# An attention and Fourier kernel: score banks taken strictly by turns, the maxima's transpose one piece later, the first pairs' row loads spread

## The chip, the core and the metric

The kernel runs on one core of a Trainium2 chip. The metric is the device time of one execution in microseconds (us). A core has five engines that run side by side, each with its own queue in order: PE (TensorE: matrix multiplies; PEld is its weight load), DVE (VectorE), ACT (ScalarE), POOL (GpSimd) and SP (SyncE, which here issues every DMA). PE writes to PSUM, which has eight banks; DVE and ACT read the results from there. A bank can be filled again only when the last reader of its earlier content is done.

## The reference

Two independent layers are computed and laid side by side in the output. Layer A is attention over 2048 positions, 32 heads of 18 channels, in 4 segments of 512, each with a softmax of its own, a linear memory carried from segment to segment, a gate per head, and an output projection. Layer B is the real part of a two-dimensional Fourier transform, written as matrix products.

```python
for s in range(N):                                   # N = 4 segments
    qs, ks, vs = q[:, :, s], k[:, :, s], v[:, :, s]
    logits = jnp.einsum("bhqd,bhkd->bhqk", qs, ks) * scale + mask
    p = _softmax(logits, axis=-1)
    a_dot = jnp.einsum("bhqk,bhkd->bhqd", p, vs)
    pq = phi(qs)
    num = jnp.einsum("bhld,bhde->bhle", pq, M)
    den = jnp.einsum("bhld,bhd->bhl", pq, z)[..., None] + 1e-6
    outs.append(g * (num / den) + (1.0 - g) * a_dot)
    pk = phi(ks)
    M = M + jnp.einsum("bhld,bhle->bhde", pk, vs)
    z = z + jnp.einsum("bhld->bhd", pk)
...
a = jnp.einsum("bsd,ed->bse", x, dft_hid_re)
b = jnp.einsum("bsd,ed->bse", x, dft_hid_im)
y = jnp.einsum("ts,bse->bte", dft_seq_re, a) - jnp.einsum("ts,bse->bte", dft_seq_im, b)
```

`mask` holds -1e9 wherever the key comes after the query, so a block of 128 rows needs only the columns up to its own.

## The kernel before

Float32 operands are split in a high and a low part, and each product is made of three. The program has three stretches. First the projections of layer A for the four segments (up to about 228 us): q, k and v go through DRAM (`qd`, `kd`, `vd`). Then, up to about 960 us, the attention of 128 heads-by-segment is woven into the matrix products of layer B. Last comes the rest of layer B and the output projection.

The weave is written out by hand. `dense()` is a generator that emits layer B a few matmuls at a time: `hidden` (L531) and `sequence` (L550), whose operands come as chunks: `c_load` (L372) issues the DMA into `craw`, `c_cut` (L380) splits it on ACT (L387, `chi`) and POOL (L392, `clo`), two chunks before `chunk` (L526) hands it to PE. `attention()` (L806) is a generator of pieces: for each step p it yields eight times, and after each piece `tick()` runs what `later(n, ...)` has put down for that tick, then as much of `dense()` is emitted as the weights in `SLOTS` (L804) ask for. So each engine's order is fixed, and all its waits are met in that order.

A pair is two heads, 2p and 2p+1; four heads (two pairs) are a group G, whose stacked rows lie in `qs_bufs[G % 4]` and `ks_bufs[G % 4]`. `stack_load(G, a, b, each)` (L419) loads rows a to b-1 of twelve, `each` of them per tick, each 72 KB. The even head of a pair first has its row minima taken (`s_fill`, three parts: PE writes scores, L665, DVE reduces them, L671), and later its transposed scores filled and turned to exponentials (`t_fill`, three parts: PE L739 to L746, ACT L749 and L750). For that the minima must become rows: `maxima(G)` (POOL, L712) cuts them in three bf16 parts, `maxima_transpose(G)` (L720) turns them on PE (tile `trm`, L722), ACT copies them out (tile `mt`, L724), and two DMAs (`qs<-mt`) write them as three more rows of the stack, in the tick after. The odd head (`f_fill`, L680) has its scores filled the plain way, exponentials by ACT (`f_exp`, L694) and the transpose by DMA (`f_turn`, L710).

One step p emits, piece by piece (the lag in pairs in brackets):

| piece | what it emits |
|---|---|
| 0 | low part of the even head's exponentials (4), `f_exp` part 2 (3), `s_fill` part 0, `f_split_hi` on ACT (3) |
| 1 | `t_fill` parts 0 and 1 (3), low split on POOL |
| 2 | for even p `maxima_transpose(p/2 - 1)`; then `s_fill` part 1, low split on DVE |
| 3 | `pv` of the even head (4), `s_fill` part 2, the mask on POOL (3) |
| 4 | `f_fill` part 1 (2), `t_fill` part 2 (3), for odd p `maxima` |
| 5 | `f_turn` (3), `stack_load` for a group to come, `f_fill` part 0 (2), `t_hi` on ACT |
| 6 | `pv` of the odd head (4), `f_fill` part 2 (2), `f_exp` part 1 (2) |
| 7 | `f_exp` part 0 (2), the output of pair p-4 |

PSUM in this stretch (pool `ps2`, L484): tag `s` has two banks (the three `s_fill` parts and `f_fill` parts 1 and 2), tag `t` has two (`t_fill`, `f_fill` part 0, `trm`), `d` three for layer B, `pv` one. With `bufs=2` under one tag the pool decides which of the two banks a fill takes. In the built program 29 of the 320 fills with tag `s` take the bank that the fill right before them had; they are all `s_fill` part 1 behind `s_fill` part 0. Among the fills with tag `t` none does.

## Time and profile before

| what | value |
|---|---|
| time of three runs | 1048.86, 1049.44, 1051.51 us (median 1049.44) |
| the profiled execution's own time | 1052.35 us |
| its span, first to last instruction | 1050.6 us |
| PE busy | 1015.7 us (97%), 9464 matmuls |
| DVE, ACT, POOL busy | 723.0, 712.7, 623.1 us |
| mean granted PE clock | 0.990 |
| DMA | 194.26 MB, 185 GB/s on average; all issued by SP |

The span is some 1.75 us shorter than the time of the same execution; the rest lies before the first and behind the last instruction. Busy times of different engines overlap. What ends up in the time is what PE, the fullest engine, does not get done: its own work, the times it stands and waits, and the stretches in which the clock granted to it is lower.

### The profile page before, as it was taken

The numbers are of one execution on the slowest core, as the hardware profiler recorded it, in microseconds if no ns is written. First come the engines' busy times: TensorE is split into PE (matmuls) and PEld (weight loads), VectorE is DVE, ScalarE is ACT, GpSimd is POOL, SyncE is SP. The second block draws the span as 40 slices with busy tenths as digits, with TensorE's granted clock in tenths as the row PEclk, the third lists the DMA queues.
The fourth block names the chain that finished last, engine by engine and source line by source line (L and its number), as shares of the span: only waits on it lengthen the run. The fifth ranks groups of instructions, "written<-read, shape, count | busy, mean of one in ns | idle before, by whom it ended". The sixth has DMA issues, their size and how long they took to land.

```text
span 1050.6 us, 25818 instructions
## 1 busy us (share of the span) xinstructions
PE 1015.7 (97%) x9464; PEld 949.4 (90%) x9464; DVE 723.0 (69%) x1903; ACT 712.7 (68%) x1654; POOL 623.1 (59%) x668
## 2 busy tenths in 40 slices
PE   9999999998999999999999999999899999999998
PEld 7989999898998999999898899999899989889998
DVE  6546556564777777878777767778677778887343
ACT  7656575653876878777787777777577766776233
POOL 3567575864765666766666766666566656766000
PEclk9999999999999999999999999999899999999999
DMA  7526164367667898999999988799999999978574
GB/s 253 177 75 208 64 206 142 118 240 173 144 159 182 181 207 202 207 196 220 206 187 209 204 174 162 155 204 199 202 209 212 216 216 212 237 148 197 142 211 140
DMA packets 287263, 194.26 MB, mean 185 GB/s; under 512 B 210208, under 2 KB 242336, under 8 KB 287136
## 3 DMA queue, kind: packets, MB, share of 16 engines
q1 hardware_dynamic: 287136, 192.61, 77.8%
q8 instruction: 74, 1.21, 0.5%
q14 instruction: 53, 0.43, 0.1%
HBM read 106.64 MB, written 43.78 MB: 143 GB/s over the span
## 4 chain that ended last, share of the span: by engine, by line
PE 73%; ACT 9%; DMA 7%; DVE 4%; POOL 3%; SPq 3%; issue 2%; POOLq 0%; ACTq 0%; DVEq 0%
PE d L494 26%; PE qk L77 6%; PE d L77 6%; PE s L665 5%; PE qk L229 5%; PE v L77 4%; DMA craw<-cT 4%; PE pv L781 3%; ACT pf L694 2%; PE d L540 2%; PE d L541 2%; PE d L542 2%; ACT hl L701 2%; PE pv L782 2%; PE m L313 2%
## 5 line engine op out<-in xcount | busy, mean ns | idle before, releaser
L671 DVE CUSTOM_DVE_ANT_0 s<-s,causal 128x128 f32<-128x128 f32 (+3 forms) x512 | 251.5, 499 | 124.1 <-PE s L665 113.0
L392 POOL TENSOR_TENSOR clo<-craw,chi 128x512 fp32r<-128x512 f32 x158 | 214.6, 1358 | 121.6 <-ACT chi L387 89.0
L494 PE MATMUL d<-wide,chi 128*128 128x288 f32 x1408 | 270.2, 309 | 0.0
L494 PEld LDWEIGHTS d<-wide,chi 128*128 128x128 f32 x1408 | 215.9, 192 | 1.3 <-issue 0.2
L494 PE MATMUL d<-wide,clo 128*128 128x288 f32 x704 | 180.8, 324 | 0.0
L705 POOL TENSOR_TENSOR hl<-pf,hl 128x768 f16<-128x768 f32 x64 | 113.2, 1768 | 79.7 <-ACT hl L701 62.5
L665 PE MATMUL s<-ks,qs 108*128 108x128 bf16 (+3 forms) x512 | 135.4, 306 | 5.9 <-DVE negm L671 4.9
L694 ACT ACTIVATE pf<-s,nb 128x128 f32<-128x128 f32 (+3 forms) x256 | 128.1, 526 | 6.2
L749 ACT ACTIVATE phi<-t 128x384 f16<-128x384 f32 x128 | 62.2, 486 | 103.2 <-PE t L746 103.2
L387 ACT ACTIVATE chi<-craw 128x512 fp32r<-128x512 f32 x160 | 100.6, 629 | 43.0 <-DMA craw<-cT 24.5
L494 PE MATMUL d<-ab,chi 128*128 128x288 f32 x640 | 126.1, 306 | 0.0
L494 PEld LDWEIGHTS d<-wide,clo 128*128 128x128 f32 x704 | 121.2, 193 | 2.7 <-issue 1.8
L764 DVE TENSOR_TENSOR plo<-pf,phi 128x384 f16<-128x384 f32 (+1 forms) x128 | 112.3, 877 | 0.0
L750 ACT ACTIVATE pf<-t 128x384 f32<-128x384 f32 (+1 forms) x192 | 100.2, 522 | 3.0 <-PE t L739 2.9
L494 PEld LDWEIGHTS d<-ab,chi 128*128 128x128 f32 x640 | 98.6, 189 | 0.8 <-issue 0.3
L701 ACT ACTIVATE hl<-pf 128x768 f16<-128x768 f32 (+1 forms) x128 | 87.4, 729 | 2.0
L540 PE MATMUL d<-wide,chi 128*128 128x288 f32 x256 | 85.2, 333 | 2.7 <-DVE wide L55 2.7
L494 PE MATMUL d<-ab,clo 128*128 128x288 f32 x320 | 84.9, 314 | 0.0
L665 PEld LDWEIGHTS <-qs 108*128 108x128 bf16 x512 | 41.4, 98 | 41.6 <-issue 25.3
L764 POOL TENSOR_TENSOR plo<-pf,phi 128x384 f16<-128x384 f32 x64 | 60.1, 940 | 31.6 <-ACT pf L750 31.1
L541 PE MATMUL d<-wide,chi 128*128 128x288 f32 x256 | 76.2, 298 | 0.0
L542 PE MATMUL d<-wide,clo 128*128 128x288 f32 x256 | 76.1, 297 | 0.0
(196 smaller groups left out, 2546.8 us busy)
## 6 DMA issues: line engine op xcount, KB each, us to landing
craw<-cT SPq DMA_DIRECT2D x128, 256.0 KB
ks<-kd SPq DMA_DIRECT2D x192, 72.0 KB
qs<-qd SPq DMA_DIRECT2D x192, 72.0 KB
craw<-xtT SPq DMA_DIRECT2D x32, 320.0 KB
out<-y SPq DMA_DIRECT2D x31, 288.0 KB
vd<-vs SPq DMA_DIRECT2D x16, 440.0 KB
vst<-vd SPq DMA_DIRECT2D x32, 220.0 KB
qd<-p SPq DMA_DIRECT2D x16, 384.0 KB
```

The lines of the kernel that those rows point to most:

```text
L77: pe.matmul(o, a, b, start=n == 0, stop=n == len(terms) - 1)
L387: act.activation(hi, raw[:, :4], AF.Copy)
L392: engine.tensor_tensor(lo, raw[:, :4], hi.bitcast(F32), OP.subtract)
L494: pe.matmul(o[h], a, b[:, h * 288:h * 288 + 288], start=start, stop=stop)
L540: pe.matmul(o, xh[:, k], wl[k][:, cs], start=k == 0, stop=False)
L665: pe.matmul(o[:, c:c + w], q[:, i * P:w], k[:, :w], start=True, stop=True)
L671: dve.tensor_tensor_reduce(o[:, c:c + w], o[:, c:c + w], CAUSAL[0][:, L - w:], scale=scale, scalar=-LOWEST, op0=OP.add, op1=OP.min, accum_ ...
L694: act.activation(f[:, FIRST_COL[i]:FIRST_COL[i] + w], o[:, c:c + w], AF.Exp, bias=nb[:, i:i + 1], scale=-1.0)
L701: act.activation(hl[:, 0, a:b], f[:, a:b], AF.Copy)
L705: engine.tensor_tensor(hl[:, 1, a:b], f[:, a:b], hl[:, 0, a:b], OP.subtract)
L750: act.activation(f[:, r:r + w], o[:, :w], AF.Exp, bias=LIFT, scale=SCALE)
L764: (pool if kind == 2 else dve).tensor_tensor(lo[:, a:b], f[:, a:b], hi[:, a:b], OP.subtract)
```

## The change

A helper `bank` takes the two banks of `s` and the two of `t` under names of their own (`s0`, `s1`, `t0`, `t1`, one buffer each) strictly by turns. All fills go through it. `maxima_transpose` moves from the head of piece 2 to the head of piece 3, behind `s_fill` part 1 and the dense work of piece 2, and ahead of `pv`; its ACT copy and its two DMAs move with it by one piece. At the start the twelve loads of group 1 go two per tick in place of three, and the first eight of group 2, which step 0 issued, are left to step 1, which loads all twelve.

```diff
@@ in the attention's pool @@
     MM, HM, BREAK = 120.0, 95.0, None
+    turns = {"s": 0, "t": 0}
+
+    def bank(name, shape, dtype, tag):
+        turns[tag] ^= 1
+        return ps.tile(shape, dtype, name=name, tag=f"{tag}{turns[tag]}", bufs=1)
@@ o_transpose @@
-        o = ps.tile([P, 4, P], F32, name="ot", tag="s")
-        e = ps.tile([P, P], F32, name="ot1", tag="t")
+        o = bank("ot", [P, 4, P], F32, "s")
+        e = bank("ot1", [P, P], F32, "t")
@@ scores @@
-        o = ps.tile([P, L], F32, name="s", tag=tag)
+        o = bank("s", [P, L], F32, tag)
@@ maxima_transpose @@
-        t = ps.tile([P, P], BF16, name="trm", tag="t")
+        t = bank("trm", [P, P], BF16, "t")
@@ t_fill @@
-        o = ps.tile([P, L], F32, name="t")
+        o = bank("t", [P, L], F32, "t")
@@ attention @@
-                stack_load(1, 0, 12, 3)
+                stack_load(1, 0, 12, 2)
...
             yield SLOTS[1]
-            if p % 2 == 0 and 0 < p <= NP:
-                maxima_transpose(p // 2 - 1)
             even(0, s_fill, 1)
             odd(F_LAG + 1, f_split_lo, dve, 0, 512)
             yield SLOTS[2]
+            if p % 2 == 0 and 0 < p <= NP:
+                maxima_transpose(p // 2 - 1)
             even(V_LAG, pv)
...
             if p % 2:
-                stack_load((p + 3) // 2, 8, 12, 2)
-            else:
+                stack_load((p + 3) // 2, 8 * (p > 1), 12, 2)
+            elif p:
                 stack_load((p + 4) // 2, 0, 8, 2)
```

## The prediction

> **What bounds the kernel now.** I read the page first. PE is busy for 1015.7 of 1050.6 us and leads the chain of waits with 73%; the next engine, DVE, has 69%. So time comes only out of what PE loses. The list of what PE waited for, longest first, names the losses:

> ```profile
> span 1050.6 us, 25818 instructions
> PE 1015.7 (97%) x9464; PEld 949.4 (90%) x9464; DVE 723.0 (69%) x1903; ACT 712.7 (68%) x1654; POOL 623.1 (59%) x668
> ...
> PE trm L722 <- ACT pf L750: 19.1, 16, 3.4
> PE s L665 <- DVE negm L671: 4.9, 6, 1.9
> PE d L540 <- DVE wide L55: 2.7, 2, 2.3
> ...
> PE s L665 <- ACT pf L694: 0.7, 2, 0.5
> PE t L739 <- DMA qs<-mt: 0.6, 1, 0.6
> ```

> The reader is to see that one small matmul, the maxima's transpose (217 ns, 32 times), stands still in 16 of 32 cases, 19.1 us in all: it takes the bank that `t_fill` part 0 filled just before, and waits for ACT's exponentials out of it. Next I looked at how the longest of these waits comes about, in the timelines of ACT and PE:

> ```profile
> 743.34 0.63 ACT L387 ACTIVATE chi<-craw 128x512 fp32r<-128x512 f32 x1 [4.18 <-DMA craw<-cT]
> 744.09 0.47 ACT L694 ACTIVATE pf<-s,nb 128x256 f32<-128x256 f32 x1
> 744.60 1.36 ACT L701 ACTIVATE hl<-pf 128x768 f16<-128x768 f32 x2
> 745.87 0.58 ACT L750 ACTIVATE pf<-t 128x512 f32<-128x512 f32 x1
> ...
> 746.49 0.27 PE L722 MATMUL trm<-ident,mb 128*128 128x128 bf16 x1 [3.44 <-ACT pf L750]
> ...
> 515.81 0.38 PE L665 MATMUL s<-ks,qs 108*128 108x128 bf16 x2 [1.88 <-DVE negm L671]
> ```

> ACT, in order, is late (here for a chunk's load), does `f_exp` part 2 and the 1.36 us of high parts, and only then frees the bank. Last the windows by engine, for the granted clock (column after POOL):

> ```profile
> 745.80:752.50 6.70, 6.01 (x44) 5.54 (x44) 3.74 (x11) 2.65 (x8) 3.67 (x3) 0.50 1.08 252
> 752.60:756.00 3.40, 3.40 (x42) 3.23 (x42) 1.73 (x6) 3.30 (x10) 2.20 (x2) 1.00 1.06 155
> 602.40:605.80 3.40, 3.40 (x17) 3.40 (x16) 2.46 (x5) 1.41 (x5) 2.90 (x4) 0.50 0.31 90
> ```

> A wait costs more than itself: after it the clock is 0.50 for 3.4 or 6.8 us. Such stretches lie at 325.9, 517.1, 602.4, 745.8 and 855.0, right behind waits of 1.83, 1.88, 2.31, 3.44 and 2.15 us, four at `trm` and one at a score fill. In them 128x288 matmuls start every 240 ns, elsewhere every 133 or 134. Start by start against the usual distance of each shape, the five lose 1.5 + 1.7 + 1.5 + 2.8 + 1.5 = 9.1 us.

> **The change, part by part**, against the profiled execution's own time, 1052.35 us (span 1050.6).

> *The transpose a piece later.* No instruction is added or removed. `trm` now has `s_fill` part 1 and the dense matmuls of piece 2 ahead of it. In groups without a wait, the time from `trm` to the `pv` behind it, its new place, is 1.4 us as a rule (277.06 to 278.41, 389.21 to 390.57; the shortest 0.3 at 450.9). Taking each wait off the start of its `pv` and comparing with the bank's release leaves 0.5 us at 942.2 and next to nothing elsewhere, except at 746.5. What then comes first is `s_fill` part 1, whose bank by turns is that of `f_fill` part 2, free when `f_exp` part 2 ends: at 744.56, while PE would arrive at 743.05, so 1.5 us stay there (and `trm` behind it finds its bank free); by the same rows 0.3 at 602 and 0.2 at 855. Of 19.1 us, 2.5 stay: -16.6. Bounds: 0 (all waits come back) to -19.1.

> *Banks by turns.* The 29 fills that took the bank just filled wait for DVE's reduction of the fill before. Of the 4.9 us on `negm`, their part is 0.3 + 1.9 + 0.6 = 2.9 us (440.7, 515.8, 878.5; under 0.1 at 409.8); the others, 2.0 us at 256, 280 and 305, already went by turns. By turns these 29 find the other bank free 0.6 us or more ahead of the fill. -2.9. Where ACT is late, turns are worse; that is counted above. For tag `t` the order of banks is what it was.

> *The clock.* All five triggers fall to 1.5 us or less. The shortest wait followed by 0.50 was 1.83 us; one of 1.74 at 942.2 was not, nor one of 2.33 at 248.9. I grant one new window (1.5): -7.6. Bounds: 0 to -9.1. [...]

> *The start.* The 2.7 us on `d L540` fall at 248.9 (2.3) and 253.5 (0.4): ACT waits 6.16 us for a chunk (`craw`, issued at 242.05, used at 247.24) whose load is behind twelve loads of group 1. In the new order on SP eight stand ahead of it; the next two chunks have six and eight fewer ahead. Four loads of 72 KB at the 206 GB/s of the window from 200 to 250 us are 1.4 us, and the later chunks gain more. -1.8, between 0 and -2.7. Group 2's loads come a step later but are first used at step 4, some 20 us on.

> *What moves with the transpose.* ACT's copy `mt` (249 ns) comes up to two ACT instructions later; `f_fill` part 0, which takes its bank, had at least 1.8 us to spare (475.7), mostly 3, so it stays clear. Both `qs<-mt` DMAs (752 ns each on SP) move past the loads of one piece: one `craw` as a rule (365 ns), some `yd<-y`; never past the transpose `ptt<-hl` (3.9 us). They now stand closer ahead of it. `t_fill` needs the rows about 9.5 us after `trm` today. Landings, read from the semaphore updates of the trace, leave 1.0 us at 502, 1.5 at 481, none at 731.7 (the one wait, 0.6), 2.3 at 546, 2.8 or more elsewhere. A shift of up to 1.9 us makes at most 0.9 + 0.4 + 1.9 = 3.2 us of waits; SP was late itself there (at 726.5 for rows ready at 722.7), so I take +1.5. Bounds 0 and 3.2.

> *A faster PE* gives ACT, DVE and SP less time. Waits of this kind that the turns don't touch are now 0.7 + 2.0 + 0.6 = 3.3 us. I let them double: +3.3. Bounds: 0 to 9.6, half of `trm`'s waits. Chunk splits (`chi`, `clo`) are 3.5 us or more ahead of their use, so layer B's operands hide this.

> Sum: -16.6 - 2.9 - 7.6 - 1.8 + 1.5 + 3.3 = -24.1, so 1052.35 - 24.1 = 1028.3, say 1028. The profiled execution is 2.9 us above the median of 1049.44. Some of that may be waits and clock that a median run has fewer of, so I don't take the sum off the median as well (1025).

> **The rivals.**

> *A: ACT stays late and the wait moves.* The reason is ACT's lateness, and `s_fill` part 1 by turns depends on the same queue. For it: the 1.5 us at 744. Against: 1.99 us lie between the end of `f_exp` part 2 and `trm`'s release (1.36 + 0.58 + 0.05), so waits under 2 us vanish. If half of 19.1 returns (7.1 more than counted) and one more window of clock: 1028.3 + 7.1 + 1.5 = 1037.

> *B: SP and the DMA engines become the bound.* By its timeline SP issues about 20 to 23 of each 25 us from 350 to 600 and 700 to 900, and the DMA share is 1.0 around 450 to 500 and 700 to 800. Against: from 750 to 800 PE had no idle time at all with DMA at 1.01. If what is won at 450 to 525 and 700 to 800 is given back (1.2 + 1.9 + 1.7 there, 4.4 + 2.8 here): 1028.3 + 12 = 1040.

> *C: short waits don't cause the low clock.* Then the four windows behind waits under 3 us remain, 6.2 us in place of the 1.5 granted: 1028.3 + 4.7 = 1033. [...]

> *D: nothing moves.* Were the bank waited for another, the list would stay: 1049 to 1050. Against: `trm` stands on the bank of `t_fill` part 0 in both programs.

> *E, slower: the rows' DMAs block SP.* SP meets its waits in order; a `qs<-mt` that waits for `mt` holds up chunks, stack loads and `ptt<-hl`. Today SP waits 7.9 us for `mt`, in 8 cases. In a group of some 20.5 us SP has about 2.5 us to spare (at 22 of 25). If each of the 32 waited longer than that, the rest would come through: at 3.5 us, 32 x 1.0 = 32 us, 1028 + 32 = 1060. It decides from 2.5 us on; one piece is 1.4, and SP's order moves by the same piece.

> **How the numbers follow.** The forecast 0.50, with a range of its own of 1020 to 1037; A 0.18, B 0.08, C 0.07, D 0.06, E 0.07; better than 1019, with all waits and clock gone (1052.35 - 19.1 - 2.9 - 9.1 - 2.7 = 1018.6), 0.04. From 1019 to 1043 leaves out D, E and the last, 0.17. No change is anything within 0.3% (3.1 us), what a measurement of this kernel can tell. Faster: forecast, A, B, C and better, 0.87; same: D, 0.06; slower: E, 0.07.

> **What would show it.** Right: the row `trm <- ACT pf` falls from 19.1 to about 1 us; `s <- DVE negm` to about 2; `s <- ACT pf` grows from 0.7 to 2 or 3; at most one clock window of 0.50 between 300 and 960; `d L540` under 1; `t <- DMA qs<-mt` about 2. Wrong: waits of 10 us or more on `s <- ACT pf` (A), PE waiting on `chi`, `clo` or `ptt` (B), windows of 0.50 behind waits of a microsecond or less (C), SP waiting over 60 us for `mt` (E).

## The result, and the profile after

The changed kernel takes 1032.4 us in the median of four runs (1031.03 to 1034.65), the kernel before 1049.61 us (1048.86 to 1051.51). The ratio is 0.9835, 95% interval 0.9813 to 0.9858: 17.2 us are gone. The profiled execution of the changed kernel took 1032.0 us with a span of 1030.3, so against the profiled execution of before (1052.35, 1050.6) it is 20.3 us.

Behind line 486 the changed kernel's lines stand 5 further down: `trm` is L727, `s` L670, `negm` L676, `f_exp` L699, the exponentials of `t_fill` L755. First the head of the page and its clock row, then the list of what PE waited for (total us, times, longest):

```profile
span 1030.3 us, 25826 instructions
PE 1006.0 (98%) x9464; PEld 940.7 (91%) x9464; DVE 719.8 (70%) x1903; ACT 713.7 (69%) x1654; POOL 625.3 (61%) x668
...
PEclk9999999999999999999999999999999999999999
```

```profile
PE s L670 <- ACT pf L699: 8.4, 10, 1.6
PE t L747 <- ACT pf L699: 3.4, 4, 1.5
PE trm L727 <- ACT pf L755: 1.8, 4, 0.7
PE s L670 <- DVE negm L676: 1.6, 2, 0.9
PE t L744 <- DMA qs<-mt: 1.5, 1, 1.5
```

The 19.1 us at `trm` are 1.8. `d L540 <- DVE wide` is no longer in the list (2.7 before). No stretch of half clock is left in the span (mean granted clock 1.000, 0.990 before), and PE's busy time fell by 9.7 us with the same 9464 matmuls. What came in return is the first two rows: PE now waits 11.8 us for ACT's `f_exp`, where it waited 0.7.

By the difference of the two lists, with the loss of each half-clock stretch counted start by start as in the prediction: `trm` -17.3, `negm` -3.3, `d` -2.7, the five half-clock stretches -9.1, rows +0.9, ACT's `f_exp` +11.1. That is -20.4, and the spans differ by 20.3.

Where the new waits come from shows in the longest of them but one. First ACT's timeline (start, us, idle before in brackets), then PE's:

```profile
711.42 0.63 ACT L387 ACTIVATE chi<-craw 128x512 fp32r<-128x512 f32 x1 [4.50 <-DMA craw<-cT]
...
713.46 0.84 ACT L699 ACTIVATE pf<-s,nb 128x128 f32<-128x128 f32 x2
714.18 0.20 ACT L696 ACTIVATE nb<-nb 128x1 f32<-128x1 f32 x1
```

```profile
714.35 0.38 PE L670 MATMUL s<-ks,qs 108*128 108x512 bf16 x1 [1.52 <-ACT pf L699]
```

ACT stood 4.5 us in front of the split of a chunk whose load had not landed. Behind it in the same queue stood `f_exp` part 1, which frees the bank that `s_fill` part 0 takes. Over the whole span ACT's waits for chunks in layer B's second product grew:

```profile
ACT chi L387 <- DMA craw<-cT: 24.5, 14, 4.2
```

```profile
ACT chi L387 <- DMA craw<-cT: 40.6, 29, 4.5
```

The first is from the kernel before, the second from the changed one. A row in ACT's list that looks like ACT's own idle time is here where PE's new rows come from.

The loads themselves are not slower. Where ACT had to wait, a load landed 4.75 us after SP began to issue it in the kernel before and 4.62 in the changed one (medians of 14 and 29). What shrank is the time that a load has: over the 128 chunks of this product, ACT is ready for the split 7.2 us after the issue before and 6.5 us after the change (means).

### The profile page after: what moved, and what is told of

Same layout as the page of the kernel before. It is cut to its first block, busy times and chain, and to the rows that moved or that the text cites. A ratio compares the mean times of both kernels' runs of the same rounds, so it can differ in the third digit from the quotient of the medians.

```text
span 1030.3 us, 25826 instructions
## 1 busy us (share of the span) xinstructions
PE 1006.0 (98%) x9464; PEld 940.7 (91%) x9464; DVE 719.8 (70%) x1903; ACT 713.7 (69%) x1654; POOL 625.3 (61%) x668
## 4 chain that ended last, share of the span: by engine, by line
PE 69%; DMA 11%; ACT 6%; SPq 6%; POOL 5%; issue 2%; DVE 1%; POOLq 0%; ACTq 0%; DVEq 0%
PE d L499 21%; DMA craw<-cT 8%; PE qk L77 6%; PE d L77 6%; PE v L77 5%; PE qk L229 5%; PE s L670 4%; PE d L545 3%; PE d L546 3%; PE d L547 3%; POOL clo L392 3%; SPq L715 2%; PE pv L786 2%; SPq L87 2%; PE look L338 2%
## 5 line engine op out<-in xcount | busy, mean ns | idle before, releaser
L676 DVE CUSTOM_DVE_ANT_0 s<-s,causal 128x128 f32<-128x128 f32 (+3 forms) x512 | 251.2, 499 | 109.9 <-PE s L670 95.3
L499 PE MATMUL d<-wide,chi 128*128 128x288 f32 x1408 | 266.5, 306 | 0.0
L499 PEld LDWEIGHTS d<-wide,chi 128*128 128x128 f32 x1408 | 212.3, 189 | 3.3 <-issue 2.2
L499 PE MATMUL d<-wide,clo 128*128 128x288 f32 x704 | 178.1, 319 | 0.0
L387 ACT ACTIVATE chi<-craw 128x512 fp32r<-128x512 f32 x160 | 100.9, 631 | 63.4 <-DMA craw<-cT 40.6
L670 PE MATMUL s<-ks,qs 108*128 108x128 bf16 (+3 forms) x512 | 133.9, 304 | 10.5 <-ACT pf L699 8.4
L699 ACT ACTIVATE pf<-s,nb 128x128 f32<-128x128 f32 (+3 forms) x256 | 128.1, 526 | 6.2
L499 PEld LDWEIGHTS d<-wide,clo 128*128 128x128 f32 x704 | 119.0, 189 | 1.8 <-issue 0.9
L755 ACT ACTIVATE pf<-t 128x384 f32<-128x384 f32 (+1 forms) x192 | 99.9, 520 | 1.3 <-PE t L744 1.3
L545 PE MATMUL d<-wide,chi 128*128 128x288 f32 x256 | 84.3, 329 | 0.0
L546 PE MATMUL d<-wide,chi 128*128 128x288 f32 x256 | 75.6, 295 | 0.0
L547 PE MATMUL d<-wide,clo 128*128 128x288 f32 x256 | 75.5, 295 | 0.0
L710 DVE TENSOR_TENSOR hl<-pf,hl 128x512 f16<-128x512 f32 x64 | 72.1, 1127 | 1.8 <-ACT hl L706 1.8
L769 POOL TENSOR_TENSOR plo<-pf,phi 128x384 f16<-128x384 f32 x64 | 62.4, 976 | 11.1 <-ACT pf L755 10.6
```

Of the source, the lines that this page charges most:

```text
L387: act.activation(hi, raw[:, :4], AF.Copy)
L499: pe.matmul(o[h], a, b[:, h * 288:h * 288 + 288], start=start, stop=stop)
L545: pe.matmul(o, xh[:, k], wl[k][:, cs], start=k == 0, stop=False)
L546: pe.matmul(o, xh[:, k], wh[k][:, cs], start=False, stop=False)
L547: pe.matmul(o, xl[:, k], wh[k][:, cs], start=False, stop=False)
L670: pe.matmul(o[:, c:c + w], q[:, i * P:w], k[:, :w], start=True, stop=True)
```

## The experiments

Each job ran the kernel before as well, and every ratio is to that job's own runs of it. Each kernel was traced once, in one of its runs, so a row can differ by a microsecond or two from what another run would show. Line numbers are those of the kernel that is shown: those of the kernel before, those of the changed kernel, or up to four more.

**The move alone.** The kernel before, with only `maxima_transpose` moved.

```diff
             yield SLOTS[1]
-            if p % 2 == 0 and 0 < p <= NP:
-                maxima_transpose(p // 2 - 1)
...
             yield SLOTS[2]
+            if p % 2 == 0 and 0 < p <= NP:
+                maxima_transpose(p // 2 - 1)
```

> The transpose moved to piece 3, banks and start as before. My theory (the move does most of it): the waits of trm on ACT pf fall from 19.1 to about 2 us and four of the five half-clock windows go (7.4 us); waits on f_exp's exponentials come back in part, as in the changed kernel (some 8 to 10 us); the fills that take the bank just filled still wait for DVE (2.9 us, one window of 1.7). Time 1034 to 1039. Rival (the strict turns are what removes the waits, the move alone only shifts them): 1043 or more, with waits of 10 us or more on s or trm and half-clock windows left.

Measured: 1036.49 us (5 runs), ratio 0.9877 (0.9856 to 0.9899), 12.2 us gained. What PE waited for:

```profile
PE s L665 <- DVE negm L671: 8.7, 12, 2.4
PE s L665 <- ACT pf L694: 4.7, 4, 1.5
PE d L540 <- DVE wide L55: 3.1, 2, 2.5
PE t L742 <- ACT pf L694: 2.4, 4, 1.3
PE trm L722 <- ACT pf L750: 2.0, 4, 0.7
```

The move alone empties the row of `trm`, and the waits for `f_exp` (4.7 + 2.4) come with it, without turns. The row on `negm` grows to 8.7, which turns then take away.

**The turns alone.** The kernel before with the helper `bank` and nothing else of the change.

```diff
-        o = ps.tile([P, L], F32, name="s", tag=tag)
+        o = bank("s", [P, L], F32, tag)
...
-        t = ps.tile([P, P], BF16, name="trm", tag="t")
+        t = bank("trm", [P, P], BF16, "t")
```

> Only the banks by turns. My theory: the 2.9 us of fills behind the bank just filled go, and with the one at 515.8 one half-clock window (1.7 us); trm waits as before. Time 1045 to 1048. Rival (by turns, a fill waits for ACT's exponentials where it could have had the bank that DVE freed): 1049 to 1053.

Measured: 1046.32 us (12 runs), ratio 0.9974 (0.9957 to 0.9992), 2.4 us gained. `trm` still waits 18.2 us in 16 cases, `negm` falls from 4.9 to 2.8, and four half-clock stretches remain.

**The start alone.** The kernel before with the row loads of the first pairs spread.

```diff
-                stack_load(1, 0, 12, 3)
+                stack_load(1, 0, 12, 2)
...
-                stack_load((p + 3) // 2, 8, 12, 2)
-            else:
+                stack_load((p + 3) // 2, 8 * (p > 1), 12, 2)
+            elif p:
```

> Only the row loads of groups 1 and 2 spread. My theory: the 2.7 us of d L540 on DVE wide near 249 and 253 and the 0.4 us at 256 go, nothing else: 1046.5 us. Rival (the later load of group 2 costs at step 4, or PE meets another wait soon): 1049 to 1050.

Measured: 1046.38 us (12 runs), ratio 0.9968 (0.9943 to 0.9993), 2.4 us gained; `d L540` falls from 2.7 to 0.4. (The traced run, 1040.56 us, was one of the fastest of the twelve; in it `trm` waits 14.4 us.) The three parts alone gain 12.2 + 2.4 + 2.4 = 17.0 us, and together 17.2: they add up, within the width of the intervals.

**Move and start, no turns.** The changed kernel with the old two-buffer tags.

```diff
-        o = bank("s", [P, L], F32, tag)
+        o = ps.tile([P, L], F32, name="s", tag=tag)
```

> The changed kernel without the turns. My theory (turns are worth their 2.9 us of waits and little more): 1034 to 1036, with 3 to 5 us of s on DVE negm and about as much s on ACT pf as in the changed kernel (8.4). Rival (strict turns cause the new waits of s on ACT pf): s on ACT pf falls to under 3 us and the time is 1027 to 1031, below the changed kernel's 1032.

Measured: 1034.09 us (4 runs), ratio 0.9862 (0.984 to 0.9885). The waits for `f_exp` are here too, 5.1 us at `s`, all of it on `s_fill` part 0, and 2.2 at `t`. So strict turns are not their cause; that rival falls.

**Load a chunk earlier.** The changed kernel, with each chunk asked for one chunk sooner.

```diff
-        c_load(n + 4)
+        c_load(n + 5)
```

> The changed kernel, with each chunk's load issued one chunk earlier (five ahead in place of four, with the same four buffers). Theory H (what PE still waits for, 11.8 us on f_exp's exponentials, 1.8 on trm, 1.5 on the rows, comes from ACT standing at the head of its queue before a split whose chunk hasn't landed, 48.9 us in all): ACT's waits for craw fall below 25 us, PE's waits on ACT pf below 7, time 1023 to 1028. Rival B (SP and the DMA engines are at their limit, so an earlier place in the queue only delays the other loads): ACT's waits for craw stay above 35 us or the rows (qs from mt) take their place, time 1031 to 1036.

Measured: 1027.14 us (6 runs), ratio 0.9802 (0.9771 to 0.9833). First PE's list, then ACT's rows on chunks:

```profile
PE t L744 <- DMA qs<-mt: 8.4, 7, 4.1
PE s L670 <- DVE negm L676: 2.0, 3, 0.9
PE pv L786 <- DMA ptt<-hl: 1.7, 3, 0.8
```

```profile
ACT chi L387 <- DMA craw<-xtT: 3.3, 3, 1.4
...
ACT chi L387 <- DMA craw<-cT: 1.3, 1, 1.3
```

ACT's waits for chunks fall from 48.9 to 4.6 us, and no wait for `f_exp` at `s` or `t` is left in PE's list. ACT is now ready for a split 9.8 us after the load's issue, on average. That settles the cause of the new waits. By the medians 5.4 us of them reach the time (1032.54 for the changed kernel in the same job). The rest comes back: the rows of the maxima (`qs<-mt`) are late instead, 8.4 us against 0.6 for the changed kernel in this job, as rival B had it, and at the longest of these waits begins a half-clock stretch of 6.8 us. The two traced runs of this pair are even equally long (1029.64 and 1029.45 us; the one is the slowest of its six, the other the fastest).

**Split later.** The changed kernel, with each split of layer B's second product placed half a chunk later in ACT's queue, so that the load has more time.

```diff
-        c_cut(n + 2)
+        if n % 80 < NT:
+            c_cut(n + 2)
...
+                if so % 4 == 2:
+                    c_cut(n + 2)
```

> The changed kernel, with each later chunk's split (ACT chi, POOL clo) emitted half a chunk later, loads unchanged. Theory H: ACT meets the split some 2 us later, so it stands less before it (craw below 25 us of ACT's waits) and PE's waits on ACT pf fall below 7 us; the parts are still about 2 us early for PE (now 3.5 or more): 1024 to 1029. Rival (ACT is late by its own work, not by the chunk): waits on ACT pf stay at 10 us or more, 1031 to 1034. If the parts come too late: a wait of PE on clo, 1036 or more.

Measured: 1027.97 us (6 runs), ratio 0.981 (0.978 to 0.984). ACT's waits for chunks fall to 26.1 us, just short of the 25 that was forecast, PE's for `f_exp` to 6.4. There is no wait for `clo`.

**Both.** The last two edits together.

> Both of the two before at once. Theory H: 1019 to 1025, PE's waits on ACT pf below 4 us. Rival B: no better than the better one of the two alone.

Measured: 1026.6 us (6 runs, 1023.73 to 1028.8), ratio 0.9799 (0.9766 to 0.9833). It is the fastest median of the study and beats both kernels. But it lies outside the 1019 to 1025 of theory H and can't be told from either cure alone, which is what rival B said: with PE's waits for `f_exp` gone, something else holds. Its list begins with

```profile
PE t L748 <- DMA qs<-mt: 7.7, 5, 4.2
PE s L674 <- DVE negm L680: 1.6, 2, 0.9
```

**The changed kernel again**, without an edit, in the job of the last three.

> The changed kernel itself beside them, for a comparison on the same chip. All theories: 1030 to 1034, no half-clock window between 300 and 960 us; if windows come back without a wait of 1.8 us or more ahead of them, the clock's part of my reasoning falls.

Measured: 1032.54 us (6 runs), ratio 0.9851 (0.982 to 0.9883). Its list has the same rows (7.3 on `f_exp` at `s`, 2.2 at `t`, 2.5 at `trm`) and ACT waits 52.2 us for chunks.

**Both, with the transpose back in its old place.** This asks what the move is worth once ACT is in time.

```diff
+            if p % 2 == 0 and 0 < p <= NP:
+                maxima_transpose(p // 2 - 1)
             even(0, s_fill, 1)
...
-            if p % 2 == 0 and 0 < p <= NP:
-                maxima_transpose(p // 2 - 1)
             even(V_LAG, pv)
```

> Loads one chunk earlier and splits half a chunk later, turns and start as in the changed kernel, but the transpose back at its old place in piece 2. If the transpose's waits came from chunks that land late (theory H), trm on ACT pf falls from 19.1 to under 7 us without the move, the rows' waits (7.7 us with both and the move) fall to under 5, and the time is 1024 to 1030. Rival (at the old place the wait is there by construction, one piece after t_fill): trm waits stay over 12 us and the time is 1032 or more.

Measured: 1039.26 us (6 runs), ratio 0.9894 (0.9857 to 0.993).

```profile
PE trm L731 <- ACT pf L759: 10.3, 11, 1.8
PE t L748 <- DMA qs<-mt: 5.9, 5, 1.8
PE pv L790 <- DMA ptt<-hl: 2.8, 3, 1.5
```

The row at `trm` lies between the two forecasts, the time is the rival's. About half of the 19.1 us at `trm` goes with ACT's lateness on chunks; the other half, 10.3 us, is there by the order of the instructions even when ACT is in time. (The halves are rough: the start alone had 14.4.) Two half-clock stretches are back as well. The move is still worth 12.7 us by the medians of two jobs, some 10 by their ratios.

**ACT frees the bank first.** The kernel just above, with the odd head's high parts (1.36 us on ACT) behind `t_fill` part 1 rather than ahead of part 0.

```diff
-            odd(F_LAG + 1, f_split_hi)
...
+            odd(F_LAG + 1, f_split_hi)
```

> The kernel of the previous pair (chunks loaded and split earlier, maxima's transpose back at the head of piece 2, 1039.3 us) with one more edit: the odd head's high parts (1.36 us on ACT) are issued behind t_fill part 1's exponentials instead of ahead of part 0's. Theory, that what remains at the transpose is by construction ACT's 1.36 us between f_exp part 2 and the release of the bank: the waits of trm for ACT pf fall from 10.3 to under 4 us, no half-clock window behind them, time 1026 to 1033, so that the move is one of two cures of the same thing. Rival, that the high parts coming later makes their low parts and the DMA transpose (ptt) late: trm's waits fall as well, but pv waits for ptt grow from 2.8 to 8 us or more and the time is 1035 or more.

Measured: 1038.13 us (6 runs), ratio 0.9887 (0.9858 to 0.9917).

```profile
PE pv L790 <- DMA ptt<-hl: 5.4, 5, 1.6
PE s L674 <- DVE negm L680: 4.7, 6, 1.6
PE trm L731 <- ACT pf L759: 3.0, 7, 0.7
PE s L674 <- ACT pf L703: 1.4, 2, 1.3
```

The theory was right on the row (`trm` 10.3 to 3.0) and wrong on the time; the rival was right on the time and too high on `ptt` (5.4). The 7.3 us came back as 2.6 at `ptt`, 3.1 at `negm` and 1.4 at `f_exp`. Here, reordering ACT passed the wait on; giving PE other work ahead of `trm` took most of it away.

**The rows' DMAs issued by ACT.** The kernel with both cures; ACT issues the two `qs<-mt` right behind its copy.

```diff
-            later(1, dma, qs_bufs[G % 4][NPAIR:NPAIR + 3, 2 * h].rearrange("c (n t) -> c n t", n=4), w[12 * h:12 * h + 12])
+            act.dma_start(qs_bufs[G % 4][NPAIR:NPAIR + 3, 2 * h].rearrange("c (n t) -> c n t", n=4), w[12 * h:12 * h + 12])
```

> As both at once (loads earlier, splits later, with the move), but the two row DMAs are issued by ACT right behind its copy mt, not by SP a tick later. If the rows come late because SP waits in order (mt 20 us of SP's waits), PE's waits on qs from mt fall from 7.7 to under 2 us and the time is 1018 to 1024. Rival (the issue costs ACT more than SP's wait cost PE, 0.75 us for each of 64): waits on ACT pf grow by more than 5 us, 1027 or more.

Measured: 1075.63 us (6 runs), ratio 1.0256 (1.022 to 1.0292), slower than before. The row on `qs<-mt` is gone from PE's list, and another leads it. Below it are three rows of SP's own list:

```profile
PE pv L790 <- DMA ptt<-hl: 43.1, 19, 4.5
```

```profile
SPq L87 <- DMA qs<-mt: 38.6, 17, 7.3
...
SPq L377 <- DMA qs<-mt: 28.5, 7, 6.7
SPq L719 <- DMA qs<-mt: 28.4, 6, 7.1
```

The theory was right on the row and wrong on the time. The rival's time of 1027 or more holds, but not its reason: PE waits for ACT's `pf` no more than 0.2 us. Neither saw what happened. SP, which no longer issues these transfers, stands 95.5 us in 30 cases until one of them has landed, before other loads (L87, L377) and before the transposes `ptt<-hl` (L719). In the longest case a load `qs<-qd` stands from 296.88 to 304.23 behind a `qs<-mt` that ACT, late in its own queue, issued only at 302.39. What ties the two queues is the program's own order of semaphores: as built, its 950 DMA instructions (886 on SP, 64 on ACT) mark eight semaphores strictly by turns, and each of the 64 on SP that stand eight places behind one of ACT's waits for that one's semaphore. In the trace of the kernel before, where all 950 are SP's, 118 or 119 mark each of the eight, and 940 wait for the semaphore that they mark. Of the 49.5 us between the spans of this kernel and the one it is made from, `pv` waiting for `ptt` is 43.1 and half clock 11.9 (13.4 against 1.5), less 7.7 of the rows: 47.3 in all.

**The clock by itself.** A kernel of bursts of 128x512 matmuls with waits of twelve lengths between them, eight of each, at changing distances.

```python
for turn in range(8):
    for steps in (1, 2, 3, 4, 5, 6, 8, 10, 12, 14, 16, 20):
        burst(56 + 3 * turn + steps % 3)
        act.activation(r, o[:, :P], AF.Copy, scale=0.012)
        for _ in range(steps):
            act.activation(r, r, AF.Copy)
        act.activation(w, r, AF.Copy)
```

> A kernel that computes nothing of the reference (its output is zeros): bursts of 57 to 79 matmuls of 128x512 in bf16, and between them PE waits for a chain of 3 to 22 copies of 128x128 on ACT, each wait length eight times at another distance. My reading of the trace of before (waits from 1.83 us on may be followed by a window of 0.50, shorter ones are not): windows of 0.50 behind a part of the waits between 1.8 and 3.4 us and behind nearly all longer ones, none behind waits under 1.7. [...] Each window behind a wait lasts 3.4 us or a multiple, and matmuls start every 427 ns in it as against 213 to 216.

Measured, by length of the wait and how many of them were followed by half clock:

| wait, us | followed by 0.50 |
|---|---|
| up to 1.79 | 0 of 24 |
| 2.13 | 3 of 8 |
| 2.47 to 2.82 | 10 of 16 |
| 3.50 to 3.72 | 6 of 8 |
| 4.2 and longer | 40 of 40 |

The length of a wait alone does not give this table: the same wait of 2.13 us did and did not cost clock. Two of them, with the 3.4 us behind each (PE's timeline, then the windows: PE busy, PEld, ACT, POOL, granted clock, DMA):

```profile
62.68 9.57 PE L57 MATMUL o<-x,w 128*128 128x512 bf16 x35 [2.13 <-ACT w L65]
...
275.81 9.45 PE L57 MATMUL o<-x,w 128*128 128x512 bf16 x42 [2.13 <-ACT w L65]
```

```profile
62.70:66.10 3.40, 3.40 (x9) 1.22 (x10) 0.00 (x0) 0.00 (x0) 0.51 0.00 0
...
275.80:279.20 3.40, 3.40 (x16) 1.58 (x17) 0.00 (x0) 0.00 (x0) 1.00 0.00 0
```

Within 3.4 us behind the one lie 9 matmuls, behind the other 16. What tells them apart is in the last section.

## Why the prediction was right, and which step was off

The forecast was 1028, the time is 1032.4, inside its own range of 1020 to 1037. Against the profiled execution, the forecast of 1028.3 missed 1032.0 by 3.7 us. Term by term:

| step of the prediction | taken | measured | from |
|---|---|---|---|
| the transpose a piece later | -16.6 | -16.2 | 19.1, less 1.8 at `trm` and 1.1 at `s_fill` part 1 |
| banks by turns | -2.9 | -3.3 | row on `negm` (0.4 of it, at 256, belongs to the start) |
| the clock | -7.6 | -9.1 | all five stretches gone, no new one |
| the start | -1.8 | -2.7 | row on `d L540` |
| what moves with the transpose | +1.5 | +0.9 | row on `qs<-mt`, 0.6 to 1.5 |
| a faster PE | +3.3 | +10.0 | 11.1 on `f_exp`, less the 1.1 above |
| sum | -24.1 | -20.4 | spans: -20.3 |

*What bounds the kernel.* Right: time came out of PE's waits and its clock, and all of it is found there.

*The step that failed is the size of "A faster PE".* The mechanism was named, but I doubled the rows that were there (0.7, 2.0 and 0.6 us) and took 3.3, with a bound of 9.6. It measured 10.0, just past the bound. That the forecast still missed by only 3.7 us is partly luck: the clock, the start, the turns and the rows came out better than I took them, by 3.4 us together, and hid half of this miss. The old rows were the wrong base. What grows is not the list of waits that PE has, but ACT's wait for chunks, 24.5 us before and 40.6 after, because a load has 0.7 us less between its issue and ACT's split (7.2 us before, 6.5 now, and 6.8 with the move alone). The loads are as fast as before, so it is the time ahead of the split that shrank; that a faster PE is what shrinks it fits these means but was not tried by itself. Before, ACT's lateness ended at `trm`, which took most of it; with `trm` out of the way the next instruction that needs ACT, `s_fill` part 0 or `t_fill` part 1, takes it. The kernel with chunks loaded earlier shows it: with ACT's wait gone, the 11.8 us on `f_exp` are gone. The prediction looked whether PE's own operands from the splits would be late (3.5 us ahead, and they never were) and not at what else stands behind a split in ACT's queue.

*Rival A* (ACT stays late, the wait moves) came about half true: 8.4 us on `s <- ACT pf`, under the 10 that was its mark (with the 3.4 at `t` it is 11.8), mostly on another fill than the one I named, and without its half-clock stretch. The time lies between the forecast and its 1037.

*Rival B* (SP and the DMA engines become the bound) was wrong by its mark: PE waits for `ptt` and the chunks' operands appear in no row. But a late load is what holds ACT, and with both cures the leading row is SP's `qs<-mt`, so SP looks like what comes next.

*Rival C* (short waits don't cause the low clock): the half-clock stretches behind the waits of 1.83 to 2.31 us are gone with those waits, which speaks for the waits as their cause. The 3 us at which this rival parts the waits no run shows as a border: in the clock kernel 13 of 24 waits between 2.1 and 2.9 us cost clock.

*Rival D* falls with the row of `trm`. *Rival E*: SP's wait for `mt` rose from 7.9 to 27.1 us in 15 cases, far from the 60 that was its mark, and PE lost 0.9 us at the rows. Nor did these waits make the chunks late: within the 8 us ahead of a late chunk's load SP waited for `mt` in 2 of 29 cases, which hold 0.7 of the 40.6 us.

## What to carry to other kernels

Before a wait is taken from the engine that bounds the kernel, follow the lateness behind it to its origin: if an in-order engine is late for a transfer, what stands behind it in that queue is late, and the next consumer takes over the wait (here 4.50 us of ACT in front of a chunk, and 1.52 us of PE for the `f_exp` behind it). What helped here was to move the origin (load sooner, split later) or to give the waiting engine independent work ahead of the wait; reordering the late engine alone passed the wait on. Neither was free: of 17.3 us taken at `trm`, 11.1 came back at `f_exp`, and with those gone 8.4 us stood at the rows. Count a short wait of PE with its clock: in the kernel before, four waits of 1.83 to 2.31 us were each followed by half clock that cost 1.5 to 1.7 us more.

## What the runs showed of the hardware

In these traces, then, it was the idle time within one cell that told which waits cost clock. Two waits of the kernel with move and start, no turns, show it (windows behind them, start and end, PE busy, PEld, DVE, ACT, POOL, granted clock, DMA, GB/s):

```profile
510.60:514.00 3.40, 3.40 (x32) 3.08 (x28) 1.77 (x8) 1.12 (x3) 1.28 (x1) 0.50 0.58 171
836.70:840.10 3.40, 3.04 (x39) 2.84 (x39) 2.40 (x5) 3.34 (x8) 2.38 (x3) 1.00 1.02 210
```

Ahead of the first lies a wait of 2.00 us (507.28 to 509.28) wholly inside a cell; ahead of the second one of 2.24 us (834.47 to 836.71), cut by the raster into 0.40 and 1.84. The shorter one cost clock. The same cut (0.83 and 1.50) explains the wait of 2.33 us at 248.9 in the kernel before, which the prediction could only note as an exception. Why the border is 2.0 us in the one kernel and 1.8 in the others stays open. Counted from the first instruction, the raster lies 1.65 us past a whole multiple of 3.413 us in the kernel before (325.91) and 2.01 past one in that with move and start (510.60). So the same waits may cost clock in one execution and none in the next, which is my estimate from these two places; that it makes up the spread of the times of before was not tried.

*SP waited for ACT's transfers.* Two small transfers per group, moved from SP's queue to ACT's, cost 0.73 us of ACT each to issue (64 of them) and made SP wait 95.5 us in 30 cases, as shown above, on semaphores that the program has both queues mark. Whether semaphores of their own would cure it was not tried.
